# Reading sixteen rows of k, v, W1 and W2 at launch, before the kernel's real loads

## The chip, the cores and the metric

The kernel runs on one core of one Trainium2 chip. The metric is the device time of the program in microseconds, where lower is better. The profile's span of the same execution is about 1.8 us shorter than that time (298.0 against 299.76 us in the profiled execution of the kernel before).

## The reference

Two stages follow each other. The first is an attention without a score matrix; the second is a feed-forward layer with an ELU.

```python
q_s = exp(q - max(q)) / sum over d          # q, k, v: 8 batches x 8 heads x 576 rows x 64, float32
k_s = exp(k - max(k)) / sum over rows
kv  = einsum('bhsd,bhse->bhde', k_s, v)     # 64 x 64 for each head
x   = einsum('bhsd,bhde->bhse', q_s, kv)    # then 4608 tokens x 512
h   = x @ w_in                              # 512 x 2048
g   = where(h > 0, h, exp(min(h, 0)) - 1)
out = g @ w_out                             # 2048 x 512
```

## The kernel before

The program adds operations with their dependences to a small scheduler. This scheduler models their times, orders every engine's instructions and emits them with semaphores. A "unit" is half of the heads of one batch, 576 KB each of q, k and v. The launch loads units 0 and 1, which make up batch 0:

```python
def program(self):
    self.init()
    sp = gp = None
    for n, h in ((0, 0), (0, 1), (1, 0), (1, 1)):   # q of unit 0 on SyncE's queue, of unit 1 on GpSimd's
        src = self.src["q"][0, 4 * h + 2 * n:4 * h + 2 * n + 2, :, :].rearrange(
            "f (p c) d -> (f p) (c d)", c=CH)
        dst = self.RQ[n][:, h, :, :].rearrange("p c d -> p (c d)")
        eng = "gp" if n else "sp"
        op = S.add(eng, ..., lambda e, src=src, dst=dst: e.dma_start(dst, src), -90, ...)
        ...
    for n, t in ((0, "k"), (0, "v"), (1, "k"), (1, "v")):
        gp = self.load(n, t, "gp", -80, follow=gp)  # all on GpSimd's queue
        ...
    for s in range(3):
        gp = self.load_w1(s, -60, follow=gp, ...)   # W1, later W2 and batch 1
    S.add("act", 1400, lambda e: e.activation(      # a first exp, so that the table load comes here
        self.RZK[0][:, :], self.RZK[0][:, :], AF.Exp), -65, X=["RZK0"])
    self.spin(10, 0)                                # matmuls on an idle tile, whose result nothing reads
    ...
```

On each unit, ScalarE applies the exp to q and k. VectorE sums q's rows, takes the reciprocal, multiplies, and casts v. TensorE transposes q, forms kv and then x. After that the large matmuls (x with W1, g with W2) run for the rest of the kernel, and the later batches are handled in between.

The softmax here doesn't subtract the row's maximum and nothing guards it: scores larger than these inputs give would overflow.

## Time and profile before

| | before |
|---|---|
| time, median of 3 runs | 299.28 us (298.98 to 299.34) |
| the profiled execution | 299.76 us, span 298.0 us |
| TensorE matmul busy | 290.4 us, 97% of the span |
| first large matmul (x with W1) | 15.06 us after the span's start |
| v of unit 1 landed | 13.43 us |

The busy lines of the profile's page, kernel before (engine, busy us, share, instructions):

```profile
PE 290.4 (97%) x1854; PEld 234.2 (79%) x1854; DVE 153.3 (51%) x188; ACT 153.9 (52%) x183; POOL 123.9 (42%) x131
```

TensorE is the limit. A change of the launch can only shift when the dense part starts, or shrink the few gaps after it. The timeline of the kernel before shows the launch. The columns are start and duration in us, engine and source line, operation, tiles, and in brackets the idle time of the engine before it with what ended it.

```profile
0.74 1.28 ACT L667 ACT_TABLE_LOAD   x1 [0.74 <-PEq L812]
...
3.72 1.36 ACT L357 ACTIVATE QR<-QR 128x576 f32<-128x576 f32 x2 [1.49 <-DMA QR<-in_q_dram]
...
4.43 1.44 DVE L363 TENSOR_REDUCE ZQ<-QR 128x9 f32<-128x576 f32 x2 [2.27 <-ACT QR L357]
...
7.48 1.54 DVE L363 TENSOR_REDUCE ZQ<-QR 128x9 f32<-128x576 f32 x2
...
12.28 0.61 DVE L468 TENSOR_TENSOR MBLK<-PS,RZK 64x128 fp32r<-64x128 f32 x2
...
13.45 0.77 DVE L406 CAST VB<-VR 128x1152 bf16<-128x1152 f32 x1 [0.56 <-DMA VR<-in_v_dram]
...
15.06 1.16 PE L558 MATMUL PS<-XT,W 128*128 128x512 f32 x4 [0.30 <-DVE RZK L463]
```

VectorE (DVE) starts when the first half of q has been through ScalarE and works until 12.89 us (12.28 + 0.61). The cast of v of unit 1 follows 0.56 us later, because v landed only then. So the data came last, by 0.56 us. The chain of waits (start us, duration us, what) says the same, and it names one more place where data counts:

```profile
4.67 8.76 DMA VR<-in_v_dram
...
13.45 0.78 DVE VB L406
...
23.45 19.23 DMA VR<-in_v_dram
...
42.70 0.78 DVE VB L406
...
43.52 0.78 PE PS L450 x67
```

The second load of v in this chain is that of unit 3. TensorE reaches the matmuls that need it at about 43 us.

In the table of short stretches (stretch, its length, busy us of each engine with instruction counts, granted clock, DMA share, GB/s), the DMA engines move less before 9 us than later:

```profile
5.00:6.00 1.00, 1.00 (x5) 0.29 (x3) 0.97 (x3) 0.42 (x2) 0.93 (x3) 1.00 0.85 281
...
7.00:8.00 1.00, 0.43 (x8) 0.38 (x8) 1.00 (x2) 0.45 (x1) 1.00 (x3) 1.00 0.99 300
...
10.00:11.00 1.00, 0.62 (x5) 0.33 (x6) 1.00 (x2) 1.00 (x3) 1.00 (x4) 1.00 1.04 424
16.00:17.00 1.00, 1.00 (x6) 0.78 (x6) 0.28 (x1) 0.50 (x1) 1.00 (x3) 1.00 1.32 387
```

The stretch from 5 to 6 us moves 281 GB/s, that from 10 to 11 us 424 GB/s. The trace's records of single packets point to a reason: some early packets take several times as long as the others (300 to 1869 ns against 178). The change is aimed at these slow packets.

### The profile page before, as it was taken

The page shows a single profiled execution, that of the slowest core. Times are in us where ns is not written, and L with a number is a line of the kernel's source. Part 1 is how long each engine was busy: PE and PEld are TensorE (multiplying, and loading weights), DVE is VectorE, ACT ScalarE, POOL GpSimd, SP SyncE. Part 2 cuts the span into 40 slices and gives each one's busy share as a digit, 9 for nine tenths or more (in the row PEclk, how much of TensorE's full clock was granted, in tenths as well). Part 3 has the DMA queues.
Part 4 walks back from the last instruction along what each step waited for, and adds up shares of the span by engine and source line. Part 5 has one row for each costly group of instructions (what it writes and reads, how often), then busy time and mean ns, then how long its engine had stood idle before and what let it go on. Part 6 is the DMA issues. An engine that isn't in the chain of part 4 may idle for free.

```text
span 298.0 us, 4418 instructions
## 1 busy us (share of the span) xinstructions
PE 290.4 (97%) x1854; PEld 234.2 (79%) x1854; DVE 153.3 (51%) x188; ACT 153.9 (52%) x183; POOL 123.9 (42%) x131
## 2 busy tenths in 40 slices
PE   7899999999999999999999999999999999999995
PEld 2388878888888888888888888888878888888883
DVE  5846952789446923683268516770662046106600
ACT  4656466963676465546554655555543354125411
POOL 8699200761277035714372228325540055005500
PEclk9999999999999999999999999999999999999999
DMA  7999987937993597039901991099002120221022
GB/s 236 388 386 389 390 291 274 369 136 88 365 216 111 182 349 167 0 104 350 246 0 29 349 295 28 0 319 219 0 0 65 29 53 0 51 55 37 0 70 70
DMA packets 36100, 49.97 MB, mean 168 GB/s; under 512 B 16496, under 2 KB 16496, under 8 KB 36080
## 3 DMA queue, kind: packets, MB, share of 16 engines
q1 hardware_dynamic: 29728, 34.28, 40.1%
q0 software_dynamic: 6032, 14.88, 15.8%
q10 hardware_dynamic: 320, 0.52, 0.5%
q8 instruction: 14, 0.23, 0.3%
q14 instruction: 6, 0.05, 0.0%
HBM read 36.70 MB, written 9.44 MB: 155 GB/s over the span
## 4 chain that ended last, share of the span: by engine, by line
PE 84%; DMA 9%; POOL 4%; DVE 1%; issue 1%; ACT 0%; POOLq 0%
PE PS L604 41%; PE PS L558 39%; DMA VR<-in_v_dram 9%; PE PS L491 3%; PE PS L450 2%; POOL W L316 1%; POOL W L327 1%; POOL KR L304 1%; DVE VB L406 1%; POOL QR L304 0%; POOL QR L654 0%; POOL VR L304 0%; ACT OSB L618 0%; POOLq L812 0%
## 5 line engine op out<-in xcount | busy, mean ns | idle before, releaser
L587 DVE SCALAR_TENSOR_TENSOR GT<-ESB,PS 128x1024 fp32r<-128x1024 f32 x69 | 83.9, 1220 | 112.8 <-POOL ESB L584 112.8
L604 PE MATMUL PS<-W,GT 128*128 128x512 f32 x576 | 140.1, 392 | 0.0
L558 PE MATMUL PS<-XT,W 128*128 128x512 f32 x576 | 132.7, 390 | 0.3 <-DVE RZK L463 0.3
L558 PEld LDWEIGHTS PS<-XT,W 128*128 128x128 f32 x576 | 107.9, 188 | 22.9 <-DVE RZK L463 0.4
L604 PEld LDWEIGHTS PS<-W,GT 128*128 128x128 f32 x576 | 106.0, 188 | 20.6
L584 POOL TENSOR_SCALAR ESB<-ESB 128x1024 f32<-128x1024 f32 x69 | 72.8, 1069 | 101.9 <-ACT ESB L572 101.9
L572 ACT ACTIVATE ESB<-PS 128x1024 f32<-128x1024 f32 x72 | 73.9, 1028 | 50.4 <-PE PS L558 50.4
L618 ACT ACTIVATE OSB<-PS 128x512 f32<-128x512 f32 x36 | 21.3, 601 | 60.2 <-PE PS L604 60.0
L403 POOL CAST VB<-VR 128x1152 bf16<-128x1152 f32 x12 | 16.4, 1364 | 43.8 <-DMA VR<-in_v_dram 43.8
L511 ACT ACTIVATE XT<-PS 128x640 fp32r<-128x640 f32 (+3 forms) x26 | 16.9, 652 | 15.0 <-PE PS L491 15.0
L363 DVE TENSOR_REDUCE ZQ<-QR 128x18 f32<-128x1152 f32 (+1 forms) x18 | 21.8, 1215 | 3.4 <-ACT QR L357 3.3
L397 ACT ACTIVATE KR<-KR 128x1152 bf16<-128x1152 f32 x16 | 18.5, 1157 | 7.6 <-DMA KR<-in_k_dram 7.6
L377 DVE TENSOR_TENSOR QS<-QR,RZQ 128x1152 f16<-128x1152 f32 x16 | 21.4, 1348 | 0.4
L357 ACT ACTIVATE QR<-QR 128x1152 f32<-128x1152 f32 (+1 forms) x18 | 18.5, 1053 | 3.8 <-DMA QR<-in_q_dram 3.8
L390 POOL CAST qsT<-QR 128x1152 fp32r<-128x1152 f16 x12 | 13.7, 1148 | 8.8 <-DMA QR<-QS 8.2
L491 PE MATMUL PS<-qsT,MBLK 128*128 128x320 f32 (+4 forms) x60 | 13.5, 306 | 0.3 <-DVE MBLK L468 0.3
L491 PEld LDWEIGHTS PS<-qsT,MBLK 128*128 128x128 f32 x60 | 11.2, 189 | 3.0 <-DVE MBLK L468 0.6
L316 POOL DMA_DIRECT2D W<-in_moe_w_in_dram x16 | 10.1, 991 | 2.4 <-DVE VB L406 2.4
L544 PE MATMUL PS<-IDLE 128*128 128x512 f16 x26 | 9.0, 479 | 1.9 <-DVE IDLE L636 1.5
L468 DVE TENSOR_TENSOR MBLK<-PS,RZK 64x128 fp32r<-64x128 f32 x32 | 9.2, 289 | 1.1
L450 PEld LDWEIGHTS PS<-VB,KR 64*64 64x64 bf16 x576 | 5.4, 107 | 3.9 <-DVE VB L406 1.8
L544 PEld LDWEIGHTS PS<-IDLE 128*128 128x128 f16 x26 | 2.7, 119 | 7.0 <-issue 2.7
(34 smaller groups left out, 59.6 us busy)
## 6 DMA issues: line engine op xcount, KB each, us to landing
out_dram<-OSB SPq DMA_DIRECT2D x68, 128.0 KB, 2.9
QR<-in_q_dram SPq DMA_DIRECT2D x12, 576.0 KB, 8.0
KR<-in_k_dram SPq DMA_DIRECT2D x12, 576.0 KB, 5.8
VR<-in_v_dram SPq DMA_DIRECT2D x12, 576.0 KB, 6.4
W<-in_moe_w_in_dram POOLq DMA_DIRECT2D x16, 256.0 KB, 8.6
W<-in_moe_w_out_dram POOLq DMA_DIRECT2D x3, 1024.0 KB, 13.2
KR<-in_k_dram POOLq DMA_DIRECT2D x4, 576.0 KB, 11.9
VR<-in_v_dram POOLq DMA_DIRECT2D x4, 576.0 KB, 13.2
```

The source lines that it names most:

```text
L357: lambda e, part=part: e.activation(part, part, AF.Exp), key,
L363: S.add("dve", 1350 if n > 1 else 750, lambda e, z=z, src=src: e.tensor_reduce(z, src, AX.X, ALU.add), key, R=self.q_res(n) if n > 1 else ...
L377: S.add("dve", 1400, lambda e: e.tensor_tensor(qso, raw[:, :, :, :], rz, ALU.mult), key, R=qR + [f"RZQ{i}"], W=[f"QS{al}"], low=True, tag= ...
L397: S.add("act", t_act(1152, False), lambda e: e.activation(ek[:, :, :, :].rearrange("p h c d -> p (h c d)"), flat, AF.Exp), key, X=[f"kR{i} ...
L491: return e.matmul(P[:, f * 512:f * 512 + n_], M[:, f, :], T[:, c0:c1, f * 64:f * 64 + 64], start=True, stop=True)
L511: S.add("act", t_act(2 * n_, True), lambda e: e.activation(dst, src, AF.Copy), key, W=names(0) + names(1), X=self.banks(ps), tag=f"evx{n}")
L558: last = e.matmul(P[:, t * 512:(t + 1) * 512], self.W1[:, kc, tt * 128:(tt + 1) * 128], self.XT[:, kc, rc:rc + BLK], start=(kc == 0), stop ...
L572: S.add("act", t_act(1024, True), lambda e: e.activation(esb[:, :], P[:, :], AF.Exp), key, W=[f"E{i}"], X=self.banks(ps), tag=f"exp{j}.{g}")
L584: S.add("gp", 1120, lambda e: e.tensor_scalar(esb[:, :], esb[:, :], 1.0, 0.0, ALU.min, ALU.max), key, X=[f"E{i}"], tag=f"min{j}.{g}", port ...
L587: S.add("dve", t_dve(1024), lambda e: e.scalar_tensor_tensor(gt, esb[:, :], -1.0, P[:, :], ALU.add, ALU.max), key, R=[f"E{i}"], W=gw, X=se ...
L604: last = e.matmul(dst, GT[:, jj, ts * 128:(ts + 1) * 128], self.W2[:, jj, :], start=(jj == 0), stop=(jj == 15))
L618: S.add("act", t_act(512, True), lambda e: e.activation(osb[:, :], src, AF.Copy), key, W=[f"O{i}0", f"O{i}1"], X=[f"b{bk}"], tag=f"evo{jb} ...
```

## The change

The touches read 64 bytes from each of sixteen rows that lie far apart in each of k and v (batch 0), W1 and W2. They go into a scratch tile that nothing reads. The intent is that whatever a first access to a far region of DRAM costs is paid by these tiny transfers, before the real loads arrive. The touches of k and v are ScalarE's first instructions; those of W1 and W2 come after q's loads on SyncE.

```diff
+        self.SEEN = a("SEEN", [16, 4, 16], F32)
...
+    def touch(self, t, eng, key):
+        i = "kv12".index(t)
+        if t in "kv":
+            src = self.src[t][0, :, :, :].rearrange("h (x s) d -> (h x) s d", x=2)[:, 0, 0:16]
+        else:
+            w = (self.w_in, self.w_out)[i - 2]
+            src = w.rearrange("(x s) d -> x s d", x=16)[:, 0, 0:16]
+        return self.S.add(eng, ISSUE[eng], lambda e: e.dma_start(self.SEEN[:, i, :], src), key,
+                          W=[f"SEEN{i}"], dma=f"tc{i}", nbytes=1024, tag=f"touch {t}")
...
         sp = gp = None
+        for t in "kv":
+            self.touch(t, "act", -99)
         for n, h in ((0, 0), (0, 1), (1, 0), (1, 1)):
...
+        for t in "12":
+            self.touch(t, "sp", -70)
         for n, t in ((0, "k"), (0, "v"), (1, "k"), (1, "v")):
             gp = self.load(n, t, "gp", -80, follow=gp)
```

## The prediction

> **What bounds the kernel now.** TensorE. In the timeline PE is dense from 15.06 us (first L558 matmuls) to 294.36; a block of 64 matmuls takes 14.51 us in the chain of waits, and the page gives PE 97% of the 298.0 us span. The change can act only on the launch (0 to 15 us) and on the one later PE gap: 0.56 us before the L450 matmuls at 43.5 us, which wait for v of unit 3 (in the chain from 23.45 to 42.68 us).
>
> The launch has two nearly equal chains. (a) DMA: v of unit 1 lands at 13.43 us; VectorE's cast of it and a small matmul group release the first L558 matmul at 15.06. (b) VectorE: q of unit 0 lands at 3.72 us, its exp ends at 4.4, and VectorE works practically without gaps until 12.89. So (b) has only 0.56 us of slack against (a).
>
> **What the touches could remove.** In the table of short stretches the DMA engines move about 320 GB/s from 2 to 9 us against about 390 later. The trace's packet records show why: 4608-byte packets of k and v take 178 ns at the median, but from 3.5 to 9.5 us a tenth of them take 300 to 1869 ns. Their excess over 178 ns, divided by 16, is 1.13 us per engine (an estimate): the most that touching k and v can win. W1's first packets (11.5 us on) show no slow ones, W2's start about five of 185 to 328 ns: touching these wins next to nothing. It is also open whether k's slow packets come from a first access at all: batch 1's k and v, just as new, show almost none at 24 to 40 us.
>
> **What they cost.** Two issues on ScalarE, about 0.5 us each (its stores at the end take 0.50 to 0.55), ahead of the 1.28 us table load. ScalarE's warm-up would end near 3.25 us instead of 2.23, still before 3.72. SyncE's two issues (0.40 us each) follow its q loads and delay nothing. The Trainium skill (DMA: Bandwidth & Descriptors, "Issuing engines are not separate DMA queues") says that all queues run on the same 16 engines; by "Why a DMA increments its semaphore by 16 and not by 1", sixteen rows go to sixteen engines. So every engine gets four 64-byte packets among q's and k's. If each takes the 0.4 us that q's own first packets take, q lands 0.1 to 0.5 us later, which eats chain (b)'s slack. A slow access is partly moved, not removed. No run here has such packets yet.
>
> **Sum.** Best case: v of unit 1 lands 0.5 to 1 us earlier, dense PE starts at most 0.5 us earlier, and the 43 us gap gives back more: about 0.9 us. Likely: 0.3 us gained. Bad case: q late, 0.3 us lost. The order of instructions should hardly change: the added operations come first, on queues with slack.
>
> Prediction: 298.9 us, 8 in 10 between 298.0 and 299.8. Faster by over 2%: 0.01; within 2%: 0.98; slower by over 2%: 0.01.
>
> **What would show it.** Right: q's first exp within 0.5 us of 3.72; v of unit 1 landing 0 to 1 us before 13.43; first L558 matmul between 14.5 and 15.3; fewer packets over 300 ns from 3.5 to 9.5 us; W1's landings unmoved; from 50 us on the chain the same, shifted. Wrong: touches that block engines for over 1 us (q lands after 4.5), or an instruction order that changed after 20 us.
>
> **What would make it wrong.** If slow accesses are costly in some executions and the profiled one was mild, touches gain more; if the altered schedule moves a load or an eviction in the steady part, several us either way.

## More of the kernel before

A spread of 1 to 2 us remains among the runs of one kernel.

## The result and the profile after

| | before | after |
|---|---|---|
| time, median of 4 runs each | 299.13 us (298.91 to 299.34) | 299.01 us (298.82 to 299.15) |
| ratio, after over before | | 0.9996, 95% interval 0.9978 to 1.0013 |
| the profiled execution | 299.76 us, span 298.0 us | 298.82 us, span 297.0 us |

A ratio is the mean time of one kernel's runs over that of the other's of the same rounds, so it is not quite the ratio of the medians. By the times no change can be seen. The order of instructions is the same on every engine except for the four added transfers. The two profiled executions nevertheless differ by 1.0 us of span, and the profile of after looks like a success. Its timeline, kernel after:

```profile
0.74 0.42 ACTq L318 DMA_DIRECT2D SEEN<-in_k_dram  x1
...
1.20 0.43 ACTq L318 DMA_DIRECT2D SEEN<-in_v_dram  x1
...
1.66 0.43 SPq L318 DMA_DIRECT2D SEEN<-in_moe_w_in_dram  x1
1.66 1.28 ACT L683 ACT_TABLE_LOAD   x1 [1.66 <-PEq L828]
...
2.95 0.20 ACT L683 ACTIVATE RZK<-RZK 128x2 f32<-128x2 f32 x1
...
3.69 2.18 ACT L369 ACTIVATE QR<-QR 128x576 f32<-128x576 f32 x3 [0.54 <-DMA QR<-in_q_dram]
...
12.22 0.61 DVE L480 TENSOR_TENSOR MBLK<-PS,RZK 64x128 fp32r<-64x128 f32 x2
...
13.08 0.77 DVE L418 CAST VB<-VR 128x1152 bf16<-128x1152 f32 x1 [0.25 <-DMA VR<-in_v_dram]
...
14.64 1.17 PE L570 MATMUL PS<-XT,W 128*128 128x512 f32 x4 [0.17 <-DVE XT L519]
```

The touches cost what was expected of their issue: 0.42 and 0.43 us on ScalarE. Its warm-up ends at 3.15 us, still before q lands, and q's exp starts at 3.69 us (3.72 before). The cast of v of unit 1 comes at 13.08 us (13.45 before) and the first large matmul at 14.64 us (15.06 before). The chain of waits of after:

```profile
4.67 8.38 DMA VR<-in_v_dram
...
13.08 0.77 DVE VB L418
...
40.72 1.88 PE PS L616 x8
42.60 0.70 PE PS L462 x66
```

The load of v of unit 1 takes 8.38 us instead of 8.76, and the gap near 43 us has closed: TensorE's own work precedes the kv matmuls, which start at about 42.6 instead of 43.52 us. A reader with only these two profiles would call the touches a gain of 1 us. The times refuse it. The profiled execution of before took 299.76 us, which is above all of the four timed runs of before (298.91 to 299.34 us). So the pair of profiles compares a slow execution of one kernel with a quick one of the other.

The packet records contain the same trap. The numbers below are worked out from the trace's DMA records. GpSimd's queue first moves 640 packets of 4608 bytes: q of unit 1, then k and v of units 0 and 1, with 128 packets each. "Excess" is the sum of (duration - 178 ns), 178 ns being the median, divided by the 16 DMA engines; it is counted for packets that start before 9.5 us. The columns by load count every packet of that load.

```
                packets   longest  excess   of it, by load (all packets):
                >= 300 ns   ns       us     q1    k0    v0    k1    v1
before             40      1869     1.13   0.66  0.32  0.15  0.02  0.07
after              25      1556     0.60   0.30  0.21  0.09  0.01  0.10
```

More than half of the excess in the kernel before belongs to q of unit 1, which no touch covers, and it falls by half all the same. That is a first hint that the touches are not the cause.

### The profile page after: what moved, and what is told of

The parts are those of the page before. It is cut to its first block, busy times and chain, and to the rows that moved or that the text cites. A ratio compares the mean times of both kernels' runs of the same rounds, so it can differ in the third digit from the quotient of the medians.

```text
span 297.0 us, 4422 instructions
## 1 busy us (share of the span) xinstructions
PE 290.4 (98%) x1854; PEld 234.3 (79%) x1854; DVE 154.0 (52%) x188; ACT 154.1 (52%) x183; POOL 123.9 (42%) x131
## 4 chain that ended last, share of the span: by engine, by line
PE 94%; DMA 3%; POOL 1%; DVE 0%; issue 0%; ACT 0%; POOLq 0%
PE PS L616 45%; PE PS L570 44%; DMA VR<-in_v_dram 3%; PE PS L503 3%; PE PS L462 2%; POOL KR L305 0%; POOL QR L668 0%; PE PS L435 0%; DVE VB L418 0%; DVE XT L519 0%; ACT OSB L630 0%; PE PS L535 0%; POOL VR L305 0%; POOLq L828 0%
## 5 line engine op out<-in xcount | busy, mean ns | idle before, releaser
L389 DVE TENSOR_TENSOR QS<-QR,RZQ 128x1152 f16<-128x1152 f32 x16 | 22.1, 1389 | 0.4
```

What stands on the lines that cost most here:

```text
L389: S.add("dve", 1400, lambda e: e.tensor_tensor(qso, raw[:, :, :, :], rz, ALU.mult), key, R=qR + [f"RZQ{i}"], W=[f"QS{al}"], low=True, tag= ...
```

## The experiments

Theory A: slow launch packets are first accesses, and touches take some of that cost away. Theory B: touches do nothing, and the difference between the profiles is chance. Theory C: the weights' touches matter. Theory D: any early small transfer helps. Every call ran its kernels on one chip together with runs of the kernel before. A correct result means within tolerance of the reference.

### The change again, with more rounds

No edit.

> The change, run again with more rounds to size an effect that the first comparison left inside its noise. Theory A (touches take part of the first-access cost of k and v out of the loads): 0.2 to 0.6 us faster than before, excess of k's and v's 4608-byte packets from 3 to 9.5 us again near 0.6 us per engine instead of 1.1. Theory B (touches do nothing; the 1.0 us between the two profiled executions is chance): ratio 1.000 within 0.0005, and the excess anywhere between 0.6 and 1.2.

Measured: 298.98 us median (298.77 to 300.76, 6 runs) against 299.05 us (298.70 to 299.87, 11 runs) for before, ratio 1.0006 (0.9981 to 1.0030). The excess was 0.72 us. The kernel before covers a whole microsecond in its own 11 runs. That fits theory B, but this run alone does not rule out a gain of a few tenths.

### The touches of k and v alone

```diff
-        for t in "12":
-            self.touch(t, "sp", -70)
```

> The touches of k and v alone. Theory A: the same time as the full change within 0.15 us, the same fewer slow k and v packets. Theory B: the time of before. Theory C (the weights' touches matter): slower than the full change by most of its gain.

Measured: 298.87 us (298.81 to 299.10, 5 runs), ratio 0.9993 (0.9977 to 1.0008), excess 0.63 us. Within the noise it is the same as the full change and the same as before.

### The touches of W1 and W2 alone

```diff
-        for t in "kv":
-            self.touch(t, "act", -99)
```

> The touches of W1 and W2 alone. Theory A: the time of before within 0.15 us; slow k and v packets as before (excess about 1.1 us per engine). Theory B: the same. Theory C: faster than before by most of what the full change gains.

Measured: 299.00 us (298.81 to 299.53, 6 runs), ratio 0.9997 (0.9982 to 1.0012). Theory C has nothing to stand on. The excess was 0.59 us, as low as in the full change, although no row of k or v was touched. Theory A expected about 1.1 here, so this run contradicts it.

### As many touches, of rows that no launch load needs

```diff
-            src = self.src[t][0, :, :, :].rearrange("h (x s) d -> (h x) s d", x=2)[:, 0, 0:16]
+            src = self.src[t][7, :, :, :].rearrange("h (x s) d -> (h x) s d", x=2)[:, 0, 0:16]
...
-            w = (self.w_in, self.w_out)[i - 2]
-            src = w.rearrange("(x s) d -> x s d", x=16)[:, 0, 0:16]
+            src = self.src["kv"[i - 2]][6, :, :, :].rearrange(
+                "h (x s) d -> (h x) s d", x=2)[:, 0, 0:16]
```

> As many touches, on the same queues at the same time, but of k and v rows of the last two batches, which no load needs at launch. Theory A: no gain, or 0.0 to 0.2 us slower than before, slow packets as before (excess about 1.1). Rival D (any small early transfer helps, by waking queues or engines): as fast as the full change and as few slow packets. Theory B: the time of before.

Measured: 299.08 us (298.55 to 299.76, 6 runs), ratio 0.9998 (0.9981 to 1.0014), excess 0.48 us. Useless touches "reduce" the slow packets further than the real ones. By these profiles it does not matter which rows are touched. Theory A falls on this and the run before; B and D remain.

### The kernel before against itself

No edit; this gives a second profile of the kernel before.

> The kernel before, unchanged, as a blind against itself: sizes the noise and gives a second profile of it. Theory B (the 1.0 us between the two profiled executions is chance, the touches do nothing): excess of the 640 launch packets of 4608 bytes 0.5 to 0.8 us per engine as in the four kernels with touches, time 298.7 to 299.1. Theory D (any small early transfer helps): excess about 1.1 again, time 299.3 or more in most executions.

Measured: 299.00 us (298.51 to 299.50, 5 runs), ratio 1.0003 (0.9991 to 1.0016). The excess was 0.43 us and the longest packet 587 ns, lower than in any kernel with sixteen-row touches, and with no touch at all. That is even below the 0.5 to 0.8 us that theory B expected. Its timeline, the unchanged kernel's second profile:

```profile
3.73 2.13 ACT L357 ACTIVATE QR<-QR 128x576 f32<-128x576 f32 x3 [1.49 <-DMA QR<-in_q_dram]
...
12.85 0.77 DVE L406 CAST VB<-VR 128x1152 bf16<-128x1152 f32 x1
...
14.45 1.16 PE L558 MATMUL PS<-XT,W 128*128 128x512 f32 x4
...
41.89 0.77 DVE L406 CAST VB<-VR 128x1152 bf16<-128x1152 f32 x1 [1.58 <-DMA VR<-in_v_dram]
...
42.71 0.78 PE L450 MATMUL PS<-VB,KR 64*64 64x65 bf16 x72
```

The cast of v at 12.85 us has no idle time before it, and the first large matmul starts at 14.45 us, earlier than in the profile of after (14.64 us). So theory D falls as well: the first profile of before was simply a slow execution.

### All launch loads from rows already read

The result is wrong on purpose.

```diff
-        src = self.src[t][b, :, :, :].rearrange(
-            "(h uf) (p c) d -> (uf p) h (c d)", h=2, c=CH)[128 * u:128 * u + 128]
+        src = self.src[t if b else "q"][b, :, :, :].rearrange(
+            "(h uf) (p c) d -> (uf p) h (c d)", h=2, c=CH)
+        src = src[128 * u:128 * u + 128] if b else src[0:128]
...
-            src = self.src["q"][0, 4 * h + 2 * n:4 * h + 2 * n + 2, :, :].rearrange(
+            src = self.src["q"][0, 4 * h:4 * h + 2, :, :].rearrange(
```

> Wrong result on purpose: after q of unit 0, the loads of q of unit 1 and of k and v of both first units read q of unit 0 once more, so that nothing they read is new. Theory A (slow launch packets are first accesses to rows): excess falls below 0.2 us per engine, v of unit 1 lands about 0.5 us earlier. Theory B2 (the slow packets come from the launch itself: queues that start, two queues at once): excess stays at 0.4 to 1.1.

Measured: 299.18 us (298.74 to 299.94, 5 runs), ratio 1.0009 (0.9996 to 1.0022). The excess was 0.79 us, with 33 packets of 300 ns or more, the longest 1854 ns. Nothing that the loads of k and v read was new (q of unit 1 began while the second half of those rows was still being read for the first time), and k and v alone still hold 0.54 us of the excess. Slow packets therefore appear without first accesses. Theory A's other forecast failed too: v of unit 1 did not land 0.5 us earlier but at 14.25 us, later than in any other profile. Its timeline:

```profile
14.27 0.76 DVE L407 CAST VB<-VR 128x1152 bf16<-128x1152 f32 x1 [0.57 <-DMA VR<-in_q_dram]
...
15.86 1.17 PE L559 MATMUL PS<-XT,W 128*128 128x512 f32 x4 [0.28 <-DVE RZK L464]
```

Two cautions remain: this kernel reads the same rows several times within a few microseconds, which could slow the loads in a way of its own, and it is one profile, of the slowest of the five executions (299.94 us). It is the reverse side of the run with the useless touches, and on the slow packets the two agree.

### A larger dose of touches: 128 rows of k and of v

```diff
-        self.SEEN = a("SEEN", [16, 4, 16], F32)
+        self.SEEN = a("SEEN", [128, 4, 16], F32)
...
-            src = self.src[t][0, :, :, :].rearrange("h (x s) d -> (h x) s d", x=2)[:, 0, 0:16]
+            src = self.src[t][0, :, :, :].rearrange("h (x s) d -> (h x) s d", x=16)[:, 0, 0:16]
...
-        for t in "12":
-            self.touch(t, "sp", -70)
```

> Touches of 128 rows of k and of v in place of 16, none of the weights. Theory A (first accesses): fewer slow launch packets than any kernel so far, excess under 0.3 us per engine. Theory B (touches do nothing): excess 0.4 to 1.1, time that of before within 0.3 us; no cost either, as the touches' packets took 8 to 11 ns each.

Measured: 299.19 us (298.83 to 299.46, 6 runs), ratio 1.0004 (0.9992 to 1.0016). The excess was 0.41 us, next to the 0.43 us that the kernel before reached without touches, so the drop below 0.3 us did not come. Eight times as many touched rows gained nothing.

### The kernel before against itself, once more

> A third profile of the kernel before. Theory B: its excess of slow launch packets falls anywhere between the 0.43 and the 1.13 us of the first two, its time between 298.5 and 299.9 us in every execution.

Measured: 299.36 us (298.97 to 299.90, 6 runs) against 299.02 us (298.60 to 299.59, 11 runs), ratio 1.0015, interval 1.0001 to 1.0030. The excess was 0.63 us. The same file against itself gave an interval that leaves out 1, so an effect of 0.15% cannot be read from a single comparison of this size. The three profiles of before have excesses of 1.13, 0.43 and 0.63 us; the six kernels with touches have 0.41 to 0.72 us. Its timeline, the unchanged kernel's third profile:

```profile
13.20 0.77 DVE L406 CAST VB<-VR 128x1152 bf16<-128x1152 f32 x1 [0.48 <-DMA VR<-in_v_dram]
...
14.77 1.16 PE L558 MATMUL PS<-XT,W 128*128 128x512 f32 x4 [0.27 <-DVE RZK L463]
```

Here VectorE waits 0.48 us for v again. So which of the launch's two chains ends last changes from execution to execution of one kernel.

The landing itself shows that the excess was also a poor measure. v counts as landed when the last of its 16 completion signals has come; in the first profile of before they came from 12.07 to 13.43 us. A mean over 16 engines does not give that last one: the 128-row touches had an excess of 0.41 us and v at 13.21 us, the second profile of before 0.43 us and v at 12.54 us. In the four kernels that touch k and v, v landed at 12.72 to 13.21 us; in the three profiles of before, with the weights' touches and with the useless ones, at 12.34 to 13.43 us. By this measure, too, the touches do nothing that can be seen.

Taken together, the timed runs of the six kernels with touches have a mean of 299.09 us (33 runs), and those of the kernel before 299.12 us (46 runs). The standard errors of the two means, worked out from the spread of the runs, are 0.07 and 0.06 us. The difference is 0.02 us with a standard error of about 0.09 us. The four kernels that touch k and v have 299.11 us alone (21 runs). These runs come from several chips, so this is a rough pooling; it makes the predicted gain of 0.3 us unlikely.

### What is an earlier v worth? One more load at launch

The remaining experiments test the other half of the prediction: what the time would do if the launch did have less, or more, to read.

```diff
+        extra = self.src["q"][7, 0:2, :, :].rearrange("f (p c) d -> (f p) (c d)", c=CH)
+        gp = S.add("gp", 1, lambda e: e.dma_start(self.ESB[3][:, 0:576], extra), -82,
+                   W=["E3"], dma="dose", nbytes=1, follow=gp, tag="dose")
         for n, t in ((0, "k"), (0, "v"), (1, "k"), (1, "v")):
```

> One more load of 288 KB on GpSimd's queue ahead of k (about 0.76 us at 390 GB/s), with the order of all other instructions kept. If DMA time at launch counts one for one, as the prediction has it: 0.6 to 0.9 us slower than before. If it is hidden: under 0.2 us.

Measured: 299.72 us (299.43 to 299.97, 5 runs), ratio 1.0024 (1.0010 to 1.0038), which is about 0.7 us slower. Its timeline:

```profile
13.65 0.77 DVE L406 CAST VB<-VR 128x1152 bf16<-128x1152 f32 x1 [0.81 <-DMA VR<-in_v_dram]
...
15.40 1.17 PE L558 MATMUL PS<-XT,W 128*128 128x512 f32 x4 [0.44 <-DVE RZK L463]
```

VectorE waits 0.81 us for v, and the dense part starts at 15.40 us (14.45 in the second profile of before). Later data costs nearly one for one.

### Less to read at launch

The result is wrong on purpose.

```diff
+        if (n, t) == (1, "v"):
+            src, dst = src[:, 0:1, :], dst[:, 0:1, :]
...
+            if i:
+                S.add("dve", 700, lambda e: e.memset(self.RAW[1]["v"][:, 1, :, :], 1.0), -7, W=["vR1"])
```

> Wrong result on purpose: half of v of unit 1 (288 KB) is not read but set to one by VectorE, so the launch has 0.76 us less to read. It bounds what a launch with fewer slow packets can win. Prediction's reasoning: dense PE starts at most 0.56 us earlier (VectorE's own chain), and the wait near 43 us shrinks too: 0.5 to 0.9 us faster. If the launch is hidden behind VectorE: under 0.3 us.

Measured: 298.99 us (298.45 to 299.44, 5 runs), ratio 0.9998 (0.9985 to 1.0012). No gain is seen, and one of 0.5 us or more is outside the interval. Its timeline:

```profile
12.75 0.76 DVE L408 CAST VB<-VR 128x1152 bf16<-128x1152 f32 x1
...
14.35 1.16 PE L560 MATMUL PS<-XT,W 128*128 128x512 f32 x4
...
40.99 0.77 DVE L408 CAST VB<-VR 128x1152 bf16<-128x1152 f32 x1 [1.58 <-DMA VR<-in_v_dram]
...
42.17 0.78 PE L452 MATMUL PS<-VB,KR 64*64 64x65 bf16 x72
```

v no longer makes anyone wait, yet the cast starts at 12.75 us, only 0.10 us before that of the second profile of before. VectorE is not free any earlier. So the 0.5 to 0.9 us for this run did not come in the times. This profile is of a quick execution, though (298.47 us; the five runs are 298.45, 298.47 and three from 298.99 us on), and in it the kv matmuls near 43 us start at 42.17 us, 0.54 us before those of the second profile of before. A gain of a few tenths stays possible.

### Less for VectorE at launch

A row sum of q is set to 64 instead of being computed. This was meant to give a wrong result, but it stays within tolerance because q is drawn with a spread of 0.1, so that the true sums of 64 exps are close to 64.

```diff
-            S.add("dve", 1350 if n > 1 else 750, lambda e, z=z, src=src: e.tensor_reduce(
+            S.add("dve", 1350 if n > 1 else 750, lambda e, z=z, src=src, cut=n == 1 and h == 1: e.memset(
+                z, 64.0) if cut else e.tensor_reduce(
```

> Wrong result on purpose: one of VectorE's 0.75 us row sums at launch is replaced by a small fill, all else and the order kept. Theory E (two balanced chains, DMA and VectorE, bound the launch; shortening one alone wins little): dense PE starts at most 0.3 us earlier than in the second profile of before (14.45 us), time within 0.25 us of before. Rival F (VectorE alone bounds the launch in an ordinary execution): dense PE starts about 0.7 us earlier and the time falls by 0.5 to 0.7 us.

Measured: 299.17 us (299.07 to 300.08, 6 runs), ratio 1.0010 (0.9996 to 1.0023). Shortening VectorE's chain by 0.7 us alone gains nothing either, so rival F falls. Its profile fell on the slowest of the six executions (300.08 us): the second half of q of unit 0 came late, ScalarE's second exp started at 5.77 us, and VectorE waited 1.56 us for it. So this profile does not show what took over in the quicker executions.

### Both

This is the edit of the two experiments above together, and the result is wrong.

> Wrong result on purpose: the shorter v load and the missing row sum together. Theory E: dense PE starts 0.6 to 0.8 us earlier (13.7 to 13.9 us) and the time falls by 0.4 to 0.7 us, more than the two edits alone add up to. Rival F: as the missing row sum alone.

Measured: 298.31 us (298.02 to 298.92, 6 runs), ratio 0.9978 (0.9965 to 0.9991), about 0.7 us faster. Its timeline:

```profile
12.21 0.77 DVE L409 CAST VB<-VR 128x1152 bf16<-128x1152 f32 x1
...
13.80 1.17 PE L561 MATMUL PS<-XT,W 128*128 128x512 f32 x4
...
41.38 0.77 DVE L409 CAST VB<-VR 128x1152 bf16<-128x1152 f32 x1 [1.68 <-DMA VR<-in_v_dram]
...
42.20 0.78 PE L453 MATMUL PS<-VB,KR 64*64 64x65 bf16 x72 [0.18 <-DVE VB L409]
```

The dense part starts at 13.80 us, 0.65 us earlier than in the second profile of before. The kv matmuls near 43 us start at 42.20 us, against 42.71 there, after a wait of 0.18 us for v of unit 3; most of the gain survives that place. Neither edit alone gained anything that could be measured; together they gain 0.7 us. Such results are the mark of two chains of nearly equal length. The times alone are thin evidence, since the unchanged kernel against itself already differed by 0.15%; the earlier starts in the profile support them.

The profiles also show where the two chains meet. In all fourteen, 254.4 to 254.5 us pass from the first kv matmul near 43 us to the end, so the start of these matmuls decides the time. Where TensorE does not wait there, they start 27.8 to 27.9 us after the first large matmul (the kernel with less to read: 42.17 - 14.35). In the second profile of before it is 28.26 us (42.71 - 14.45), because v of unit 3 came last by the chain of waits: its cast starts at 41.89 us, with 40.99 us in the kernel with less to read and 41.38 us here. So in that execution the reads that counted were those up to v of unit 3, and not those up to v of unit 1. This also explains why less work for VectorE alone need not gain anything, but the slow profile of that run does not show it.

This is no usable kernel, as half of v is missing; no run here points to a correct version that shortens both chains.

## Why the prediction was right or wrong

- **The time: right, but it supports no mechanism.** 298.9 us was predicted, with 298.0 to 299.8; 299.01 us was measured. The range also holds the 299.13 us of the kernel before, so a change without any effect would have hit it as well. The expected gain itself did not show.
- **TensorE bounds the kernel and only the launch can move: right.** The instruction order was unchanged except for the four transfers, as predicted.
- **"The most that touching k and v can win" is 1.13 us: wrong in its attribution.** The 4608-byte packets from 3.5 us on were taken for k and v. The first 128 of them are q of unit 1, and in the profile of before they hold 0.66 us of the excess. k and v together hold 0.56 us (0.32 + 0.15 + 0.02 + 0.07). The prediction also took one profile for the kernel: two more profiles of the same kernel gave 0.43 and 0.63 us. And it took the mean over 16 engines for the delay of a load, which the landings do not follow (13.21 us with an excess of 0.41, 12.54 us with 0.43).
- **"Likely: 0.3 us gained": not found.** The pooled difference is 0.02 us with a standard error of 0.09. The step that failed is the assumption that touches take over part of the slow accesses. Touches of other rows (0.48 us of excess), of the weights (0.59) and no touches (0.43, 0.63) leave as few slow packets as the real touches (0.60, 0.72), and rows already read still give 0.79. The prediction named this doubt itself, from batch 1's loads. That touching W1 and W2 wins next to nothing was right.
- **"q lands 0.1 to 0.5 us later": wrong.** q's first exp started at 3.69 us, against 3.72 before. Each of the 64 touch packets is recorded with 8 to 11 ns, not the 0.4 us of q's first packets. The Trainium skill (DMA: Bandwidth & Descriptors, "Issuing engines are not separate DMA queues") has all queues share the DMA engines. The runs do not contradict that; the shared time was merely too small to see. That sixteen rows go to sixteen engines (same page, "Why a DMA increments its semaphore by 16 and not by 1") no run here shows: the trace has 16 records and 16 completion signals for each touch, which fits, but they carry no engine number.
- **ScalarE's warm-up "near 3.25 us": right.** It ended at 3.15 us and stayed hidden behind q's landing.
- **Two chains, with 0.56 us of slack for VectorE's: right in kind, and more binding than said.** In the slow profiled execution v came last. In the second profile VectorE came last and v of unit 1 causes no wait, but v of unit 3 does near 43 us; in the third v of unit 1 came last again, by 0.48 us. The lighter v load gains nothing measurable, and with both chains shortened the 0.7 us appears. The best case of 0.9 us was probably out of reach for touches even if they had removed every slow packet; no run tests that directly.
- **The signs that were to show it right came true in the profile of after, all but one:** v earlier by 0.38 us, dense matmuls at 14.64 us, fewer slow packets. (W1's landings were to stay unmoved; the first came at 13.71 us instead of 14.12.) They came true for another reason, since the unchanged kernel shows them too in its second profile (v at 12.54 us, dense matmuls at 14.45 us, 26 slow packets instead of 40). A sign that the unchanged kernel can also give supports nothing.

What causes the slow packets stays open. They are not removed by touching, they appear without new rows, and their number varies between executions of one kernel.

## What to carry to other kernels

Before believing a cause seen in a pair of profiles, profile the unchanged kernel again; here its own excess of slow packets ranged from 0.43 to 1.13 us, wider than the supposed effect. To test a warming transfer, send it to useless addresses: if that "helps" as much, the addresses are not the cause. Where two chains end within half a microsecond of each other, shorten both in one experiment, because shortening either alone may show nothing. And find the last place where the chains meet: here it is near 43 us, long after the launch.

## What the Trainium skill lacked or had wrong

- No page of it says whether a first access to a DRAM region costs anything. The runs found no sign of such a cost: loads of k and v from rows already read keep 0.54 us of excess per DMA engine, against 0.56 in the first profile of before. The touches' packet records of 8 to 11 ns do not settle it, because these touches landed 2.5 to 3.9 us after their issue, so the records leave most of that time out.
- DMA: Bandwidth & Descriptors, "Latency and other measured facts", gives HBM access as 0.2 us on average and 2 us under high load. No run here checks these figures, since a packet's record is not that latency (8 to 11 ns for a touch). The page lacks that at launch about 3 to 6% of the packets (19 to 40 of 640) take 300 to 1869 ns where the median takes 178 ns, and that their number varies between executions of one kernel (26 to 40 over three profiles).
- DMA: Bandwidth & Descriptors, "SWDGE vs HWDGE vs iDMA", says that a packet has preferably at most 4096 bytes. On GpSimd's queue two runs of 2304 bytes stand as one record of 4608 bytes (q of unit 1: 256 rows in 128 records), while SyncE's queue records the same kind of row as 2304 bytes each. Whether a record is a packet in the page's sense is not shown. Counting loads by packet size without knowing this probably led to the wrong attribution above.
